# A decode layer's last weight matrix in five transfers instead of nine, and four more of its tiles in the last tile's banks

## The chip, the cores and the metric

One core of a Trainium2 chip runs the whole kernel. The metric is device time in microseconds for one execution, as the median of several. "us" is microseconds throughout.

## The reference

One token of a transformer layer with attention and a gated feed-forward part side by side, all in fp32:

```python
xn = layernorm(x)                                  # x: 1 x 1 x 1024
# A: sliding-window attention over a cache
q = (xn @ wq)                                      # 32 heads of 128
k, v = last 4096 rows of k_cache, v_cache          # 4 kv heads, each for 8 query heads
o = softmax(q k^T * 128 ** -0.5) v
a = o.reshape(1, 1, 4096) @ wo                     # 4096 x 1024
# B: gated feed-forward
h = gelu(xn @ w_gate) * (xn @ w_up)                # 3584 hidden values
b = h @ w_down                                     # 3584 x 1024
return x + a + b
```

There is one row of activations, so every weight is read once and used for one vector: 94.38 MB of weights and cache come in from memory for an output of 1024 numbers.

## The kernel before

All weights and the cache pass through one SBUF buffer, `ring`, of 176 KB in each of the 128 partitions. `pieces` (line 234) lists the transfers in order: kind, which part, the place in the ring in KB, and the size in KB. `pump` (271) issues the next piece on SyncE's queue as soon as no piece that is still in use (`live`) covers its place; `done` frees a place and pumps again. All transfers of weights therefore stand in one queue, in the order of the list. `Program` (36) records every operation with what it reads and writes, and derives the semaphore waits from the overlap of these ranges; a transfer into a place waits for the last readers of exactly that range.

The kinds are q, k, v, g, u, o and d, for wq, the key cache, the value cache, w_gate, w_up, wo and w_down. The change concerns d. w_down's 3584 rows are laid out so that partition p holds rows 28 p to 28 p + 27; tile t is the t-th of these in every partition, a 128 x 1024 block of 4 KB a partition. There are 28 tiles, 0 to 27. Tile t has to be multiplied by column t of the hidden vector and summed over the partitions. There are four ways to take a tile in:

- `tile_on_dve` (644): VectorE multiplies the tile by the column as a per-partition factor and adds it to `out_part` in SBUF (128 x 1024). The sum over the partitions comes later.
- `tiles_on_rows` (611): TensorE, four tiles side by side in four column groups of 32, into all of `acc`, two PSUM banks of 512 columns.
- `tile_on_pe` (626): TensorE, one tile as four matmuls of 256 columns, one in each column group, into `sums`.
- `half_on_pe` (636): TensorE, half a tile as four matmuls of 128 columns, one in each column group, into the first 128 columns of one of `acc`'s banks; half 0 goes to bank 0 and half 1 to bank 1.

`contract` (648) takes one piece: the tiles that are not in `dve_tiles` go to TensorE, those in it to VectorE, and at the end `done` frees the place. `HID_A` to `HID_D` (30 to 33) are the tiles within a piece that VectorE takes. A matmul is recorded as two MATMUL and two LDWEIGHTS records in the trace, so a tile in `sums` is eight records and a half tile is eight as well.

Each engine works through its own instructions in the order in which they are written. The end of the kernel, in that order: both halves of wo and tiles 0 to 11 of w_down by `tiles_on_rows` and VectorE; the sum of `acc` into `out_part`; tiles 12 to 23 by `tile_on_pe` and VectorE; tile 24; `out_part` itself, summed over the partitions by the matrix `unit` in the same way; tile 25, which closes `sums`; VectorE's add of `sums` to x in `x_out`; tile 26 in halves; and then tile 27, whose two halves are transferred separately. After each half of 27 VectorE adds `acc`'s bank to `x_out` and two small transfers store that half of the output.

Of the kernel before, what the change touches and what calls it, by code (L numbers as in the profile page):

```python
# [11 lines left out]
D = 1024  # L12
# [15 lines left out]
HEADS_A = [0, 2, 4, 6, 8, 10, 12, 14]  # L28
HEADS_B = [0, 2, 4, 6, 8, 10, 12, 14]
HID_A = [0, 2, 4, 6, 8]  # L30
HID_B = [1, 3, 5, 7]
HID_C = []
HID_D = [1]


class Program:
# [110 lines left out]
def decode_layer(nc, x, k_cache, v_cache, wq, wo, w_gate, w_up, w_down, out):  # L147
    prog = Program(nc)

    def sbuf(name, *shape):  # L150
        return nc.alloc_sbuf_tensor(name, list(shape), F32)
# [4 lines left out]
    def mm(o, lhsT, rhs, start, stop, parts=None):  # L156
        prog.add(
            "pe", lambda e: e.matmul(o, lhsT, rhs, start=start, stop=stop),  # L158
            [lhsT] + (parts or [rhs]), [o],
        )  # L160
# [16 lines left out]
    def dve(call, reads, writes, engine="dve"):  # L177
        prog.add(engine, call, reads, writes)
# [9 lines left out]
    def add(o, a, b):  # L188
        dve(lambda e: e.tensor_add(o, a, b), [a, b], [o])  # L189
# [38 lines left out]
    def heads_of(a):  # L228
# [12 lines left out]
    ]  # L241
    held = {}

# [35 lines left out]
    def done(*key):  # L279
        del live[key]  # L280
        pump()
# [32 lines left out]
    unit = sbuf("unit", P, 64)  # L314
# [133 lines left out]
    p = rows_sb[:, 0, :]  # L448
# [152 lines left out]
    out_part = part[:, :D]  # L601
# [3 lines left out]
    def column(t):  # L605
        return hz[:, 32 * t:32 * t + 64]
# [4 lines left out]
    def tiles_on_rows(pairs):  # L611

        for at in range(0, len(pairs), 4):
            group = pairs[at:at + 4]
            for f in range(2):
                for k, (z, w) in enumerate(group):
                    c = (state["turn"] + k) % 4
                    first = (c, f) not in state["rows"]
                    state["rows"].add((c, f))
                    mm(  # L620
                        acc[32 * c:32 * c + 32, f, :], z[:, 31:63], w[:, f * NQ:(f + 1) * NQ],
                        first, state["turn"] + k >= state["total"] - 4,
                    )
            state["turn"] += len(group)

    def tile_on_pe(wide, w, stop=False):
        blocks = w.rearrange("p (f c n) -> p c f n", f=2, c=4)
        for c in range(4):
            at = 31 * (c % 2)
            mm(  # L630
                sums[32 * c:32 * c + 32, :].rearrange("p (f n) -> p f n", f=2),
                wide[:, at:at + 32], blocks[:, c], state["fresh"], stop,
            )
        state["fresh"] = False

    def half_on_pe(wide, w, half, first, last):
        for c in range(4):
            at = 31 * (c % 2)
            mm(
                acc[32 * c:32 * c + 32, half, :P],  # L640
                wide[:, at:at + 32], w[:, half * NQ + c * P:half * NQ + (c + 1) * P], first, last,
            )

    def tile_on_dve(z, w):
        add_scaled(out_part, w, z[:, 31:32], state["part"])
        state["part"] = False

    def contract(kind, i, z, dve_tiles, rows):
        w = held[kind, i].rearrange("p (t n) -> p t n", n=D)
        count = w.shape[1]  # L650
        rest = [(z(t), w[:, t, :]) for t in range(count) if t not in dve_tiles]
        if rows:
            tiles_on_rows(rest)
        else:
            for pair in rest:
                tile_on_pe(*pair)
        for t in dve_tiles:
            tile_on_dve(z(t), w[:, t, :])
        done(kind, i)
# [41 lines left out]
    contract("o", 1, lambda t: head(TO + t), HEADS_B, True)  # L701
    contract("d", (0, 12), column, HID_A, True)
    add(out_part, acc[:].rearrange("p a n -> p (a n)"), out_part)
    contract("d", (12, 20), lambda t: column(12 + t), HID_B, False)
    contract("d", (20, 22), lambda t: column(20 + t), HID_C, False)
    contract("d", (22, 24), lambda t: column(22 + t), HID_D, False)
    tile_on_pe(column(24), held["d", (24, 25)])
    tile_on_pe(unit[:], out_part)
    tile_on_pe(column(25), held["d", (25, 26)], True)
    add(x_out[:].rearrange("p f n -> p (f n)"), sums[:], x_out[:].rearrange("p f n -> p (f n)"))  # L710
    for half in range(2):
        half_on_pe(column(26), held["d", (26, 27)], half, True, False)
    stores = out.rearrange("a b (f c n) -> (a b) f c n", f=2, c=4)
    for half in range(2):
        half_on_pe(column(27), held["d", (27, 28)], half, False, True)
# [32 lines left out]
```

## Time and profile before

| | us |
|---|---|
| median of 3 runs | 226.8 |
| lowest and highest | 226.49, 226.84 |
| the profiled execution, in all | 226.83 |
| its span | 225.5 |
| TensorE busy | 87.5 |
| VectorE busy | 143.2 |
| ScalarE busy | 26.3 |

The span reaches from the first to the last instruction of the program; the rest of the time lies around it. PE stands for TensorE's matmuls and PEld for its weight loads, DVE for VectorE, ACT for ScalarE, SP for SyncE, which issues the transfers; SPq is the issuing itself. Times in the profile are counted from the start of the span. In a row of the timeline stand the start, the duration, the engine, the line, the operation, what it writes and reads, its shape, and how often it comes; in brackets stands the idle time of the engine before it and what ended it. Rows of matmuls overlap, so the duration of a row is that of the group. In a row of the windows stand the stretch, its length, the busy time of each engine with its number of instructions (PE, PEld, DVE, ACT, POOL), the clock that was granted to TensorE as a share of the full one, the busy share of the DMA engines, and GB/s.

### The profile page before, as it was taken

What the parts mean: (1) busy time and instruction counts of PE and PEld (TensorE: products, weight loads), DVE (VectorE), ACT (ScalarE), POOL (GpSimd) and SP (SyncE); (2) the same over time, 40 slices, a digit from 0 to 9 for tenths busy, and PEclk for the clock granted to TensorE, in tenths of its full rate; (3) what the DMA queues carried; (4) which work ended last, traced back from release to release, by engine and by line L of the source; (5) the groups of instructions that cost most, each with busy time, mean ns of one, the idle gap of its engine ahead of it and who ended that gap; (6) DMA issues with size and microseconds to landing.
All of it is one profiled execution on the core that took longest, in us unless ns stands there. A gap on an engine that the chain in (4) does not pass through costs nothing.

```text
span 225.5 us, 1396 instructions
## 1 busy us (share of the span) xinstructions
PE 87.5 (39%) x574; PEld 34.8 (15%) x574; DVE 143.2 (64%) x127; ACT 26.3 (12%) x45; POOL 0.7 (0%) x6
## 2 busy tenths in 40 slices
PE   1200000007699007989002537137339204408475
PEld 0100000006263002462000111011002001002131
DVE  7500998499727990000998699869538804938691
ACT  2000000004555001482000300200000000000000
POOL 1000000000000000000000000000000000000000
PEclk9999999999999755999755667857855855965889
DMA  9899899899989999999999998999999999999992
GB/s 373 372 395 535 372 395 535 349 405 478 468 349 426 465 401 503 427 397 471 427 397 392 433 509 387 478 391 491 419 395 488 419 395 413 427 439 442 382 405 111
DMA packets 3317, 94.46 MB, mean 419 GB/s; under 512 B 350, under 2 KB 366, under 8 KB 1008
## 3 DMA queue, kind: packets, MB, share of 16 engines
q1 hardware_dynamic: 3288, 94.38, 97.5%
q8 instruction: 4, 0.07, 0.1%
q10 hardware_dynamic: 24, 0.01, 0.0%
q14 instruction: 1, 0.01, 0.0%
HBM read 94.38 MB, written 0.00 MB: 419 GB/s over the span
## 4 chain that ended last, share of the span: by engine, by line
DMA 65%; DVE 26%; PE 7%; issue 1%; SPq 1%; DVEq 0%
DVE part L213 24%; DMA ring<-in_B_w_down 19%; DMA ring<-in_A_wq 18%; DMA ring<-in_B_w_gate 15%; DMA ring<-in_A_wo 13%; PE acc L158 3%; PE tp L163 2%; PE s_p L158 2%; DVE part L209 1%; SPq L219 1%; DVE rows_sb L186 0%; DVE part L189 0%; DVEq L118 0%; SPq L118 0%
## 5 line engine op out<-in xcount | busy, mean ns | idle before, releaser
L213 DVE SCALAR_TENSOR_TENSOR part<-ring,xz,part 128x3584 f32<-128x3584 f32 (+1 forms) x19 | 78.8, 4148 | 26.6 <-DMA ring<-in_B_w_gate 22.6
L163 PE MATMUL tp<-ident,ring 128*128 128x128 f32 x128 | 20.3, 303 | 44.4 <-DMA ring<-in_A_k_cache 42.8
L213 DVE SCALAR_TENSOR_TENSOR part<-ring,oz,part 128x1024 f32<-128x1024 f32 x15 | 19.3, 1285 | 9.9 <-DMA ring<-in_A_wo 9.4
L172 ACT ACTIVATE ring<-tp 128x512 f32<-128x512 f32 x32 | 18.1, 596 | 58.4 <-PE tp L163 58.0
L163 PEld LDWEIGHTS tp<-ident,ring 128*128 128x128 f32 x128 | 15.0, 152 | 51.2 <-DMA ring<-in_A_k_cache 42.9
L209 DVE TENSOR_SCALAR part<-ring,xz 128x3584 f32<-128x3584 f32 (+1 forms) x3 | 6.5, 2176 | 19.7 <-DMA ring<-in_A_wq 12.1
L158 PE MATMUL acc<-ring,oz 128*32 128x512 f32 x64 | 11.7, 899 | 16.8 <-DMA ring<-in_A_wo 16.8
L213 DVE SCALAR_TENSOR_TENSOR part<-ring,hz,part 128x1024 f32<-128x1024 f32 x10 | 12.8, 1285 | 6.1 <-DMA ring<-in_B_w_down 5.8
L158 PE MATMUL acc<-part,unit 128*32 128x448 f32 (+1 forms) x48 | 7.3, 742 | 22.3 <-DVE part L213 22.3
L158 PE MATMUL o_p<-ring,pT 128*32 128x512 f32 x64 | 11.0, 847 | 7.1 <-DMA ring<-in_A_v_cache 6.5
L158 PE MATMUL acc<-ring,hz 128*32 128x128 f32 (+1 forms) x60 | 8.0, 616 | 10.1 <-DMA ring<-in_B_w_down 10.1
L158 PE MATMUL s_p<-ring,qz 128*32 128x512 f32 x64 | 9.3, 598 | 0.0
L163 PE MATMUL tp<-ident,rows_sb 128*128 128x128 f32 x16 | 3.5, 361 | 12.0 <-ACT rows_sb L172 11.8
L158 PE MATMUL sums<-ring,hz 128*32 128x256 f32 x72 | 6.2, 482 | 4.7 <-DMA ring<-in_B_w_down 4.7
L158 PEld LDWEIGHTS acc<-ring,oz 128*32 128x32 f32 x64 | 2.5, 155 | 26.6 <-DMA ring<-in_A_wo 19.4
L158 PEld LDWEIGHTS acc<-part,unit 128*32 128x32 f32 x48 | 1.4, 126 | 26.4 <-DVE part L213 24.2
L172 ACT ACTIVATE rows_sb<-s_p,negm 128x512 f32<-128x512 f32 x2 | 1.4, 687 | 30.4 <-DVE negm L209 30.4
L158 PEld LDWEIGHTS o_p<-ring,pT 128*32 128x32 f32 x64 | 2.6, 149 | 14.5 <-issue 13.4
L158 PE MATMUL acc<-ring,xz 128*32 128x448 f32 x32 | 4.8, 767 | 0.0
L158 PEld LDWEIGHTS acc<-ring,hz 128*32 128x32 f32 x60 | 2.2, 135 | 15.8 <-issue 14.0
L163 PEld LDWEIGHTS tp<-ident,rows_sb 128*128 128x128 f32 x16 | 2.3, 179 | 15.5 <-ACT rows_sb L172 13.6
L158 PEld LDWEIGHTS sums<-ring,hz 128*32 128x32 f32 x72 | 2.4, 136 | 9.2 <-DMA ring<-in_B_w_down 7.3
(85 smaller groups left out, 47.8 us busy)
## 6 DMA issues: line engine op xcount, KB each, us to landing
ring<-in_B_w_gate SPq DMA_DIRECT2D x2, 7168.0 KB, 31.9
ring<-in_B_w_up SPq DMA_DIRECT2D x2, 7168.0 KB, 33.9
ring<-in_A_k_cache SPq DMA_DIRECT2D x2, 4096.0 KB, 39.7
ring<-in_A_v_cache SPq DMA_DIRECT2D x2, 4096.0 KB, 34.8
ring<-in_B_w_down SPq DMA_DIRECT2D x1, 6144.0 KB, 42.9
ring<-in_B_w_down SPq DMA_DIRECT2D x1, 4096.0 KB, 38.8
ring<-in_B_w_down SPq DMA_DIRECT2D x2, 1024.0 KB, 40.4
ring<-in_B_w_down SPq DMA_DIRECT2D x3, 512.0 KB, 42.0
```

What stands on the lines that cost most here:

```text
L158: "pe", lambda e: e.matmul(o, lhsT, rhs, start=start, stop=stop),
L163: prog.add("pe", lambda e: e.transpose(o, i, eye), [i, eye], [o])
L172: "act", lambda e: e.activation(o, i, func, scale=scale, **kw),
L209: dve(lambda e: e.tensor_scalar(o, i, s1, s2, op0=op0, **kw), reads, [o])
L213: lambda e: e.scalar_tensor_tensor(o, i, factor, other, op0=ALU.mult, op1=ALU.add),
L219: engine, lambda e: e.dma_start(o, i), list(reads), list(writes), dma=True, tag=tag
```

## The change

w_down's pieces are cut anew. Before, they are of 48, 32, 8, 8, 4, 4, 4 and 4 KB a partition, the last in two halves: nine transfers. After, they are of 48, 44, 16 and 4 KB, the last in two halves: five. They cover the same places in the ring. The piece of 44 KB holds tiles 12 to 22, of which VectorE takes two (12 and 14) and TensorE nine, in `sums`; before, VectorE took five of tiles 12 to 23. `out_part` then closes `sums`. Tiles 23 to 26 come as one piece, and go in halves into `acc`'s banks, all four into half 0 and then all four into half 1, ahead of tile 27. Tiles 24 and 25 went into `sums` before, 23 to VectorE, and 26 into `acc`'s banks already.

```diff
-HID_B = [1, 3, 5, 7]
-HID_C = []
-HID_D = [1]
+HID_B = [0, 2]
...
-        ("d", (0, 12), 128, 48), ("d", (12, 20), 0, 32), ("d", (20, 22), 32, 8),
-        ("d", (22, 24), 40, 8), ("d", (24, 25), 48, 4), ("d", (25, 26), 52, 4),
-        ("d", (26, 27), 56, 4), ("d", (27, 28), 60, 4),
+        ("d", (0, 12), 128, 48), ("d", (12, 23), 0, 44), ("d", (23, 27), 44, 16),
+        ("d", (27, 28), 60, 4),
...
-    contract("d", (12, 20), lambda t: column(12 + t), HID_B, False)
-    contract("d", (20, 22), lambda t: column(20 + t), HID_C, False)
-    contract("d", (22, 24), lambda t: column(22 + t), HID_D, False)
-    tile_on_pe(column(24), held["d", (24, 25)])
-    tile_on_pe(unit[:], out_part)
-    tile_on_pe(column(25), held["d", (25, 26)], True)
+    contract("d", (12, 23), lambda t: column(12 + t), HID_B, False)
+    tile_on_pe(unit[:], out_part, True)
     add(x_out[:].rearrange("p f n -> p (f n)"), sums[:], x_out[:].rearrange("p f n -> p (f n)"))
+    wide = held["d", (23, 27)].rearrange("p (t n) -> p t n", n=D)
     for half in range(2):
-        half_on_pe(column(26), held["d", (26, 27)], half, True, False)
+        for t in range(23, 27):
+            half_on_pe(column(t), wide[:, t - 23, :], half, t == 23, False)
```

## The prediction

> **What bounds the kernel now.** I read the page first: its head, the busy shares, the transfer queues and the shares of the chain that ended last.
>
> ```profile
> span 225.5 us, 1396 instructions
> PE 87.5 (39%) x574; PEld 34.8 (15%) x574; DVE 143.2 (64%) x127; ACT 26.3 (12%) x45; POOL 0.7 (0%) x6
> q1 hardware_dynamic: 3288, 94.38, 97.5%
> DMA 65%; DVE 26%; PE 7%; issue 1%; SPq 1%; DVEq 0%
> ```
>
> One queue of transfers keeps the 16 DMA engines 97.5% busy over the whole span. No compute engine is near that; TensorE works for 39% of the time. So the time is the stream of 94.38 MB, plus what still has to be done after its last byte. The chain of waits in order of time shows how short that remainder is:
>
> ```profile
> 180.50 42.73 DMA ring<-in_B_w_down
> 223.23 0.04 issue
> 223.28 0.47 PE acc L158 x8
> 223.75 0.02 issue
> 223.77 0.29 DVE part L189
> ```
>
> The last piece of w_down lands at 223.23. Half a tile on TensorE follows, then one add of 0.29 that ends at 224.06, and 1.4 us later the span ends. The change rewrites just this tail, so I took the timeline of the last 40 us, TensorE's rows first, then VectorE's and the weight loads whose spacing gives TensorE's pace:
>
> ```profile
> 203.63 6.50 PE L158 MATMUL acc<-ring,hz 128*32 128x512 f32 x28 [9.33 <-DMA ring<-in_B_w_down]
> 213.25 4.26 PE L158 MATMUL sums<-ring,hz 128*32 128x256 f32 x48 [3.12 <-DMA ring<-in_B_w_down]
> 218.22 0.64 PE L158 MATMUL sums<-ring,hz 128*32 128x256 f32 x8 [0.71 <-DMA ring<-in_B_w_down]
> 219.49 0.64 PE L158 MATMUL sums<-ring,hz 128*32 128x256 f32 x8 [0.62 <-DMA ring<-in_B_w_down]
> 219.94 0.62 PE L158 MATMUL sums<-part,unit 128*32 128x256 f32 x8
> 220.78 0.64 PE L158 MATMUL sums<-ring,hz 128*32 128x256 f32 x8 [0.21 <-DMA ring<-in_B_w_down]
> 222.03 1.04 PE L158 MATMUL acc<-ring,hz 128*32 128x128 f32 x24 [0.61 <-DMA ring<-in_B_w_down]
> 223.28 0.43 PE L158 MATMUL acc<-ring,hz 128*32 128x128 f32 x8 [0.21 <-DMA ring<-in_B_w_down]
> 203.59 6.57 DVE L213 SCALAR_TENSOR_TENSOR part<-ring,hz,part 128x1024 f32<-128x1024 f32 x5 [4.00 <-DMA ring<-in_B_w_down]
> 213.30 6.57 DVE L213 SCALAR_TENSOR_TENSOR part<-ring,hz,part 128x1024 f32<-128x1024 f32 x5 [1.82 <-DMA ring<-in_B_w_down]
> 213.68 0.20 PEld L158 LDWEIGHTS sums<-ring,hz 128*32 128x32 f32 x4 [0.23 <-issue]
> ...
> 216.24 0.80 PEld L158 LDWEIGHTS sums<-ring,hz 128*32 128x32 f32 x16 [0.23 <-issue]
> ```
>
> Three things are in these rows. First, landings: a wait on w_down ends at 203.6 (tiles 0 to 11), 213.25 (12 to 19), 218.22 (22, 23), 219.49 (24), 220.78 (25), 222.03 (26) and 223.28 (second half of 27). Second, TensorE idles before each and keeps up. Third, it has two paces. A tile in "sums" is eight records, two passes of four that run side by side in the four column groups. From 213.25 to 216.24 a pass takes 2.99 / 7 = 0.427; 24 records then remain of the 48 that end at 217.51, less than 1.3 us for five passes. The windows row by row show why:
>
> ```profile
> 188.98:192.39 3.41, 3.39 (x16) 0.79 (x20) 3.27 (x3) 0.00 (x0) 0.00 (x0) 0.50 1.03 447
> 192.39:195.80 3.41, 1.91 (x20) 0.36 (x12) 3.30 (x4) 0.00 (x0) 0.00 (x0) 1.00 1.00 432
> ...
> 202.62:206.04 3.42, 2.41 (x12) 0.68 (x16) 2.42 (x2) 0.00 (x0) 0.00 (x0) 0.50 0.98 422
> 206.04:209.45 3.41, 3.41 (x17) 0.87 (x12) 3.30 (x4) 0.00 (x0) 0.00 (x0) 0.50 0.98 423
> 209.45:212.86 3.41, 0.68 (x6) 0.00 (x0) 1.93 (x2) 0.00 (x0) 0.00 (x0) 1.00 0.89 377
> 212.86:216.28 3.42, 3.03 (x32) 1.42 (x36) 2.90 (x3) 0.00 (x0) 0.00 (x0) 0.50 1.00 413
> 216.28:219.69 3.41, 2.08 (x36) 0.78 (x32) 3.34 (x3) 0.00 (x0) 0.00 (x0) 1.00 1.02 405
> 219.69:223.10 3.41, 2.55 (x48) 0.85 (x40) 0.60 (x2) 0.00 (x0) 0.00 (x0) 1.00 0.53 202
> ```
>
> The columns that matter are the first, PE busy, and the granted clock (0.50 or 1.00). The clock steps at 192.39, 209.45, 212.86 and 216.28, all on one grid of 3.41 us. A stretch with TensorE busy for 3.03 of 3.42 (89%) is followed by full clock, one with 2.41 (71%) is not; a stretch with 0.68 (20%) is followed by half clock. So every burst after a long wait begins at half clock: the full clock came 3.03 us after the start in the burst of 213.25 (at 216.28), and 5.82 after it in that of 203.63 (at 209.45). In the kernel before, the slow stretch is over well ahead of the last landing.
>
> **The change part by part.**
>
> Transfers. Nine become five. Eight tiles in one transfer land 213.25 - 203.6 = 9.65 after the one before, 1.21 a tile; tiles sent alone land 1.27, 1.29 and 1.25 apart (218.22, 219.49, 220.78, 222.03). The second transfer, now 11 tiles, is therefore whole at 203.6 + 11 x 1.21 = 216.9; taking the pace of the pieces, (218.22 - 213.25) / 4 = 1.24 a tile, 217.25. I take 216.9, since this too is one large transfer. Tiles 23 to 26 land at 216.9 + 4.85 = 221.75, and the last half about 1.25 later, at 223.0: 0.2 earlier than now. That is all that fewer transfers can give, 4 x 0.06. A rule in the Trainium skill, "DMA: Bandwidth & Descriptors", section "Anatomy of one DMA", puts about 2.0 us of fixed cost on each transfer (measured there on GpSimd's path). By it, as an estimate, four fewer would be worth 8 us were they serial; the spacing of 1.25 to 1.29 for 512 KB says that here it runs beside the data of the next.
>
> Issue. SyncE now waits for the reader of tile 10 of the first half of wo before the second transfer, not of tile 6, two VectorE steps of 1.3 later. What is queued behind it:
>
> ```profile
> 170.42 9.21 DVE L213 SCALAR_TENSOR_TENSOR part<-ring,oz,part 128x1024 f32<-128x1024 f32 x7
> 174.37 17.02 SPq L219 DMA_DIRECT2D ring<-in_B_w_down  x8
> ring<-in_B_w_down SPq DMA_DIRECT2D x1, 4096.0 KB, 38.8
> ```
>
> Issue near 177 instead of 174.4 against bytes that cannot flow before 203.6: nothing, with 26 us of cover. Four issues fewer on SyncE: nothing, as none was late.
>
> VectorE. It has two of tiles 12 to 22 instead of five of 12 to 23: 2 x 1.3 = 2.6 from 216.9, done at 219.5. The "unit" matmuls that fold its sum in stand behind nine tiles on TensorE, later than that at any clock below. No cost; but the work it loses goes to TensorE.
>
> TensorE. After the landing at 216.9 it gets nine tiles and the unit tile in "sums" (ten of 256 columns), then eight half tiles for 23 to 26 and two for 27, all of 128 columns. Before, it had only tile 26 and 27 in halves and idle gaps of 0.2 to 0.7 between tiles. At full clock a tile of eight records takes 0.64 alone and a half 0.43 alone; the difference, 0.21, is one half's streaming, so a tile streams 0.43 and a half 0.21 to 0.22, with 0.21 of latency once. (The tile at 219.49 and the unit at 219.94 are 0.45 apart.) All of it at full clock: 10 x 0.43 + 10 x 0.22 = 6.5 us. From 216.9 that ends at 223.4. The stream for 27's second half now ends at 223.28 + 0.22 = 223.5. So even at full clock the new order is only level with the old one: the 0.2 from the transfers is used up.
>
> The clock. TensorE stops near 210.1 (203.63 + 6.50) and waits until 216.9, 6.8 us, which holds at least one whole stretch of 3.41 with no work. The one after 209.45, with 20%, was enough for half clock, so the burst starts at half clock. Each microsecond there does 0.215 / 0.427 of its full-clock work, so it costs 0.495. How long does it last? The traced bounds are 3.03 and 5.82 us. If the grid lay as it does here, the stretch 216.28 to 219.69 would be busy for 82%, between the 71% that failed and the 89% that passed: 2.8 us or 6.2. Nothing in one trace fixes the grid against the landing in another execution, so I take the middle of the two bursts, 4.4 us, and 2.8 and 6.2 as ends. Cost 4.4 x 0.495 = 2.2, ends 1.4 and 3.1. The Trainium skill, "TensorE: Matmul & The Clock Gate", "The HAM clock gate", agrees on the step and its 3413 ns, calls the window free-running (no single trace can show that), and wants at least one busy window. Read as a wholly busy window, an average start would wait 5.1 us, an estimate of 2.5 and a time of 229.3; the 89% stretch that was followed by full clock says that less is enough.
>
> No wait for data is left in it. Tiles 23 to 26 land at 221.75 and are wanted when the ten tiles of "sums" are through, at the earliest 216.9 + 4.3 + 1.4 = 222.6. The halves of 27 land at 222.4 and 223.0 and are wanted 8 x 0.22 = 1.8 later than that, at 224.4. VectorE's add of "sums" follows the unit tile and runs beside the halves.
>
> The end. The two final adds were 0.63 apart and now follow halves 0.22 apart; the first takes 0.29, so the second waits 0.07.
>
> Sum against the profiled execution: the last half's stream ends at 216.9 + 6.5 + 2.2 = 225.6 instead of 223.5, plus 0.07: +2.15 us. The profiled execution took 226.83 in all (span 225.5 and 1.33 around it), 0.03 above the median 226.8. So 226.83 + 2.15 = 229.0 us.
>
> **The rivals.**
>
> TensorE at full clock. If the burst ran at 1.00 from the start, the stream ends at 223.4 for 223.5 and the last add waits 0.07: 226.8, no change. For it: the full clock survived 192.39 to 195.80 with 1.91 us of work. Against it: 20% in 209.45 to 212.86 lost the clock at once, and here the wait is 6.8 us.
>
> The stream still decides (the other side). If TensorE finished "sums" and the eight halves before 223.0, the last landing would end the kernel again, 0.24 earlier: 226.83 - 0.24 = 226.6. That needs the landing of 12 to 22 at or before 216.4, or under 6 us of work where 6.5 is counted at full clock; both would have to differ from the rows. The fixed cost that the Trainium skill states above would be this rival with a larger price, 218.8 by its estimate; the spacing of 1.25 leaves that almost no chance.
>
> The clock never rises in the burst. Then 20 passes of 0.427 and 20 of 0.214 take 12.8 us, 6.3 more: 233. For it only the 5.82 us of the burst at 203.63; every burst that filled one whole stretch got its clock.
>
> **How the numbers follow.** Forecast (TensorE ends the kernel after a half-clock start of 2.8 to 6.2 us): 0.90, time 229.0. Full clock: 0.04, 226.8. The stream decides: 0.03, 226.6. Never full: 0.03, 233. What this kernel's timing can tell from no change is about 0.2%, 0.45 us. Faster 0.03, same 0.04, slower 0.93. The forecast's ends are 226.83 - 0.1 + 0.07 + 1.4 = 228.2 and, with 3.1, 229.9. The later landing of 217.25 adds 0.35 at the top. A share just over 71% that passes (2.4 us of half clock, cost 1.2) takes 0.2 off at the bottom, and 0.1 is left for the rounding of the terms. Range 227.9 to 230.2.
>
> **What would show it.** In the profile after: a wait on w_down that ends near 216.9; a TensorE burst from there without a gap over 0.2 to the last add, 8 to 10 us long; granted clock 0.50 in its first 2.8 to 6.2 us; weight loads 0.43 apart there; the last add released by TensorE and not by a landing; TensorE, not the transfers, in the last 7 us of the chain. Wrong would be: idle TensorE ahead of the last half, a burst at 1.00 from the start, or halves that stream in well over 0.22.

## The result, and the profile after

| | before | after |
|---|---|---|
| median of 5 runs, us | 226.8 | 229.34 |
| lowest and highest | 226.46, 226.84 | 228.68, 229.67 |
| the profiled execution, its span | 226.83, 225.5 | 228.68, 227.3 |

The ratio of after to before is 1.0113, with a 95% interval of 1.0092 to 1.0133: slower by 2.5 us. The times of the kernel after are also wider apart, by 1.0 us instead of 0.4. Line numbers after are two lower: L156 is the helper for matmuls, L187 that for adds.

The head of the page, and the part of the chain of waits that belongs to the tail:

```profile
span 227.3 us, 1483 instructions
q1 hardware_dynamic: 2712, 94.37, 96.6%
```

```profile
176.70 39.81 DMA ring<-in_B_w_down
216.51 0.04 issue
216.56 6.50 PE sums L156 x80
223.05 2.02 PE acc L156 x72
225.07 0.02 issue
225.10 0.51 DVE part L187 x2
```

Before, the chain was in a transfer until 223.23. Now it leaves the transfers at 216.51, and TensorE holds it for the last 8.5 us before the two final adds. The timeline shows the burst without a gap, and the weight loads its two paces:

```profile
216.56 6.07 PE L156 MATMUL sums<-ring,hz 128*32 128x256 f32 x72 [7.82 <-DMA ring<-in_B_w_down]
222.45 0.60 PE L156 MATMUL sums<-part,unit 128*32 128x256 f32 x8
222.88 2.36 PE L156 MATMUL acc<-ring,hz 128*32 128x128 f32 x80
...
216.98 0.20 PEld L156 LDWEIGHTS sums<-ring,hz 128*32 128x32 f32 x4 [0.23 <-issue]
...
219.97 0.20 PEld L156 LDWEIGHTS sums<-ring,hz 128*32 128x32 f32 x4 [0.23 <-issue]
220.40 1.74 PEld L156 LDWEIGHTS sums<-ring,hz 128*32 128x32 f32 x32 [0.23 <-issue]
```

Passes come 0.43 apart until 220.40 (seven steps from 216.98 to 219.97); from there four tiles' weight loads (32) take 1.74, 0.22 a pass. In the windows on this execution's grid (behind the length PE's busy time, behind POOL's column the granted clock):

```profile
210.37:213.79 3.42, 0.00 (x0) 0.00 (x0) 0.73 (x1) 0.00 (x0) 0.00 (x0) 1.00 0.98 422
213.79:217.20 3.41, 0.65 (x8) 0.40 (x12) 0.59 (x1) 0.00 (x0) 0.00 (x0) 0.50 0.90 384
217.20:220.61 3.41, 3.41 (x38) 1.58 (x32) 1.97 (x2) 0.00 (x0) 0.00 (x0) 0.50 0.94 386
220.61:224.03 3.42, 3.42 (x90) 2.35 (x84) 0.42 (x1) 0.00 (x0) 0.00 (x0) 1.00 0.16 56
```

The stretch from 210.37 had no work, so the clock is 0.50 from 213.79; the burst starts at 216.56, fills the stretch from 217.20 whole, and has 1.00 from 220.61: 4.05 us at half clock.

### The profile page after: what moved, and what is told of

The parts are those of the page before. It is cut to its first block, busy times and chain, and to the rows that moved or that the text cites. A ratio compares the mean times of both kernels' runs of the same rounds, so it can differ in the third digit from the quotient of the medians.

```text
span 227.3 us, 1483 instructions
## 1 busy us (share of the span) xinstructions
PE 90.5 (40%) x622; PEld 37.5 (17%) x622; DVE 139.2 (61%) x124; ACT 26.2 (12%) x45; POOL 0.7 (0%) x6
## 4 chain that ended last, share of the span: by engine, by line
DMA 72%; DVE 17%; PE 10%; ACT 1%; issue 0%; DVEq 0%
DMA ring<-in_A_v_cache 18%; DMA ring<-in_B_w_down 18%; DVE part L211 14%; DMA ring<-in_B_w_gate 14%; DMA ring<-in_A_wo 13%; DMA ring<-in_A_wq 10%; PE o_p L156 5%; PE sums L156 3%; DVE part L207 2%; PE acc L156 1%; PE tp L161 1%; ACT rows_sb L170 0%; DVE m L199 0%; ACT pT L170 0%; DVE part L187 0%
## 5 line engine op out<-in xcount | busy, mean ns | idle before, releaser
L156 PE MATMUL acc<-ring,oz 128*32 128x512 f32 x64 | 11.2, 868 | 17.2 <-DMA ring<-in_A_wo 17.2
L156 PE MATMUL acc<-part,unit 128*32 128x448 f32 (+1 forms) x48 | 9.8, 967 | 20.3 <-DVE part L211 20.3
L156 PE MATMUL o_p<-ring,pT 128*32 128x512 f32 x64 | 11.8, 907 | 7.9 <-DMA ring<-in_A_v_cache 7.2
L211 DVE SCALAR_TENSOR_TENSOR part<-ring,hz,part 128x1024 f32<-128x1024 f32 x7 | 9.0, 1284 | 9.7 <-DMA ring<-in_B_w_down 9.5
L156 PE MATMUL acc<-ring,hz 128*32 128x128 f32 (+1 forms) x108 | 7.8, 428 | 8.7 <-DMA ring<-in_B_w_down 8.7
L156 PE MATMUL s_p<-ring,qz 128*32 128x512 f32 x64 | 9.3, 598 | 0.0
L156 PE MATMUL sums<-ring,hz 128*32 128x256 f32 x72 | 6.1, 512 | 7.8 <-DMA ring<-in_B_w_down 7.8
L156 PEld LDWEIGHTS acc<-ring,oz 128*32 128x32 f32 x64 | 2.5, 153 | 26.5 <-DMA ring<-in_A_wo 19.5
L156 PEld LDWEIGHTS acc<-part,unit 128*32 128x32 f32 x48 | 1.8, 159 | 25.8 <-DVE part L211 22.3
L156 PEld LDWEIGHTS acc<-ring,hz 128*32 128x32 f32 x108 | 3.6, 121 | 13.0 <-issue 12.8
L156 PE MATMUL acc<-ring,xz 128*32 128x448 f32 x32 | 5.6, 870 | 0.0
L156 PEld LDWEIGHTS o_p<-ring,pT 128*32 128x32 f32 x64 | 2.8, 159 | 15.6 <-issue 14.5
L156 PEld LDWEIGHTS sums<-ring,hz 128*32 128x32 f32 x72 | 2.8, 147 | 11.5 <-DMA ring<-in_B_w_down 8.7
```

Of the source, the lines that this page charges most:

```text
L211: lambda e: e.scalar_tensor_tensor(o, i, factor, other, op0=ALU.mult, op1=ALU.add),
```

## The experiments

The theory: the large landing lets TensorE idle long enough to lose its clock, and then gives it 6.5 us of full-clock work at once, of which the first 2.8 to 6.2 us run at half clock. Rival A: it is the work that was moved to TensorE (fewer tiles on VectorE, more halves), the clock aside. Rival B: TensorE waits for pieces that land too late. Each kernel below was timed against the kernel before on the same chip (226.81 for e1 to e4, 226.69 for e5, e7, e8 and e9, 226.56 in a single run for e10), and each ratio is to that kernel.

**e1: keep TensorE busy ahead of the landing.**

```diff
     add(out_part, acc[:].rearrange("p a n -> p (a n)"), out_part)
+    for _ in range(6):
+        for c in range(4):
+            mm(s_p[32 * c:32 * c + 32, :], unit[:, 31:63], rows_sb[:, 0, :], True, True)
```

> The changed kernel, with six groups of 24 matmuls in all into an unused bank (no data that is in transfer) behind tiles 0 to 11, so that TensorE does not idle ahead of the large landing. Theory (the half-clock start of the long burst is the cost): granted clock 1.00 over the whole burst, the last passes end 6.5 us after the landing, 226.6 to 227.0 us. Rival A (TensorE simply has more work behind a later landing, the clock aside): no gain, 229.3. Rival B (the large pieces land too late, and TensorE waits for them): no gain, 229.3.

227.9 us, ratio 1.0057 (1.0038 to 1.0076), and two clusters: 227.37, 227.40, 227.46 and 228.34, 228.50, 228.70. So 1.4 of the 2.5 us came back at the median and 1.9 in the lower cluster, where the theory had all of it. The profiled execution (227.46) is of the lower cluster. Its TensorE rows show that the clock was kept, and what was overlooked:

```profile
209.36 5.74 PE L156 MATMUL s_p<-rows_sb,unit 128*32 128x512 f32 x47
216.84 4.09 PE L156 MATMUL sums<-ring,hz 128*32 128x256 f32 x72 [1.74 <-DMA ring<-in_B_w_down]
220.75 0.61 PE L156 MATMUL sums<-part,unit 128*32 128x256 f32 x8
221.73 2.39 PE L156 MATMUL acc<-ring,hz 128*32 128x128 f32 x80 [0.36 <-DMA ring<-in_B_w_down]
```

The nine tiles take 4.09 instead of 6.07, and then TensorE waits for tiles 23 to 26, which land together at 221.7. After that it has ten halves, 2.2 us of streaming, which end at 223.9. In the kernel after, whose burst is slow, this second wait does not show. For the upper cluster the guess was that six groups are too few when the burst of tiles 0 to 11 gets its clock early: they end early, and TensorE idles again. No profile of the upper cluster was taken. e7 tests both.

**e2: the same matmuls, three groups, in the kernel before.**

> The kernel before with three such groups of matmuls behind tiles 0 to 11: what they cost by themselves. Theory: the stream of transfers ends this kernel, TensorE has slack at either clock, 226.8 within 0.3. If the extra matmuls disturb the stream or its landings, slower than 227.1; if the clock held the kernel before back as well, faster than 226.4.

226.8 us, ratio 0.9999 (0.9991 to 1.0008). The three groups cost nothing by themselves. In the profile the clock is at 1.00 from the landing of tiles 12 to 19 (213.24) and back at 0.50 from 219.47 (its rows stand in the last section), and the time is the same: the kernel before has nothing to gain from the clock.

**e3: nine transfers with the new split of work.**

```diff
-        ("d", (0, 12), 128, 48), ("d", (12, 23), 0, 44), ("d", (23, 27), 44, 16),
-        ("d", (27, 28), 60, 4),
+        ... the nine of before ...
+    tiles = [held["d", (22, 24)][:, D:]] + [held["d", (t, t + 1)] for t in range(24, 27)]
+    for t in range(23, 27):
+        for half in range(2):
+            half_on_pe(column(t), tiles[t - 23], half, t == 23, False)
```

> The nine transfers of before with the work split as in the changed kernel (two of tiles 12 to 22 on VectorE, 23 to 26 in halves into acc's banks, tile by tile as they land). Theory: the split alone costs nothing as long as tiles land one by one, since the last landing still ends it, 226.6 to 227.1. Rival A (the split, with five tiles' worth of work moved to TensorE or to halves, is the cost): 228.5 to 229.3.

226.75 us, ratio 1.0 (0.9992 to 1.0009). The split costs nothing by itself: rival A alone falls. Its burst also ran at half clock, from 213.1 to 216.5, but it started 3.6 us earlier (212.98), and the tiles that land one by one leave gaps to catch up in:

```profile
212.98 5.78 PE L156 MATMUL sums<-ring,hz 128*32 128x256 f32 x72 [4.57 <-DMA ring<-in_B_w_down]
...
221.78 1.05 PE L156 MATMUL acc<-ring,hz 128*32 128x128 f32 x24 [0.62 <-DMA ring<-in_B_w_down]
223.05 0.43 PE L156 MATMUL acc<-ring,hz 128*32 128x128 f32 x8 [0.21 <-DMA ring<-in_B_w_down]
```

**e4: five transfers with the old split.**

```diff
-HID_B = [0, 2]
+HID_B = [1, 3, 5, 7]
...
+    tile_on_dve(column(23), wide[:, 0, :])
+    tile_on_pe(column(24), wide[:, 1, :])
+    tile_on_pe(unit[:], out_part)
+    tile_on_pe(column(25), wide[:, 2, :], True)
     for half in range(2):
-        for t in range(23, 27):
-            half_on_pe(column(t), wide[:, t - 23, :], half, t == 23, False)
+        half_on_pe(column(26), wide[:, 3, :], half, True, False)
```

> The five transfers of the change with the work split of before (VectorE takes 13, 15, 17, 19 and 23; 24 and 25 go into sums, 26 in halves). Theory: the burst still starts at half clock at the late landing and VectorE's five tiles end near 223.2, so unit, 25, 26 and 27 follow them: 224.9 for the last stream, 228.3 to 228.8. Rival A (the split is the cost, not the transfers): 226.6 to 227.0.

228.74 us, ratio 1.009 (1.0077 to 1.0103). With the work where it was, the five transfers still cost 1.9 us: here VectorE is the one that starts late, as its timeline and the wait of the unit tile show. TensorE's clock has no part in this loss, for TensorE idles 1.13 us ahead of the unit tile. So what costs is the late landing of many tiles at once, for whichever engine gets them.

```profile
216.72 6.57 DVE L211 SCALAR_TENSOR_TENSOR part<-ring,hz,part 128x1024 f32<-128x1024 f32 x5 [5.46 <-DMA ring<-in_B_w_down]
...
223.34 0.64 PE L156 MATMUL sums<-part,unit 128*32 128x256 f32 x8 [1.13 <-DVE part L211]
```

**e7: as e1, eight groups.**

> The changed kernel with eight groups of extra matmuls behind tiles 0 to 11 instead of six, so that TensorE's idle time ahead of the large landing stays under half a stretch of 3.41 us in every execution. Theory: the two clusters of e1 (227.4 and 228.5) are executions in which the clock was kept and in which it fell again; now it is always kept, 227.3 to 227.6, spread under 0.4. What is left over before (0.6) is TensorE waiting for tiles 23 to 26, which land together at 221.7: ten halves of 0.22 after that. Rival (the upper cluster is something else, for instance the extra matmuls running into the burst): still two clusters, median 227.9 or later.

227.36 us (227.24 to 227.61), ratio 1.0028 (1.0017 to 1.0039). One cluster: the upper one of e1 is gone, and the spread is 0.4 instead of the 1.0 of the kernel after. That e1's upper cluster was the clock is argued from this; no trace shows it. With the clock kept the loss is 0.7 us (against 226.69), so 1.9 of the 2.5 us are back. The windows of the burst, all at 1.00, and TensorE's rows with the wait that is left:

```profile
211.61:215.02 3.41, 3.41 (x40) 1.16 (x35) 0.00 (x0) 0.00 (x0) 0.00 (x0) 1.00 0.80 340
215.02:218.43 3.41, 2.85 (x42) 1.13 (x38) 1.35 (x2) 0.00 (x0) 0.00 (x0) 1.00 0.97 413
218.43:221.85 3.42, 3.09 (x60) 1.58 (x51) 1.49 (x2) 0.00 (x0) 0.00 (x0) 1.00 0.72 283
```

```profile
217.00 4.09 PE L156 MATMUL sums<-ring,hz 128*32 128x256 f32 x72 [0.56 <-DMA ring<-in_B_w_down]
220.91 0.61 PE L156 MATMUL sums<-part,unit 128*32 128x256 f32 x8
221.88 2.39 PE L156 MATMUL acc<-ring,hz 128*32 128x128 f32 x80 [0.36 <-DMA ring<-in_B_w_down]
```

**e8: as e7, with the piece of 23 to 26 cut in two.**

```diff
-("d", (23, 27), 44, 16),
+("d", (23, 25), 44, 8), ("d", (25, 27), 52, 8),
```

Each pair goes into both halves before the next pair.

> As e7, with the piece of tiles 23 to 26 cut into two of 8 KB a partition (six transfers). Theory: tiles 23 and 24 now land 2.4 us earlier and are done before 25 and 26 land, so TensorE ends level with the stream, 226.7 to 227.1, 0.4 to 0.6 less than e7. Rival (the wide piece does not matter, the rest over before is work on TensorE): as e7, 227.4.

226.84 us, ratio 1.0006 (0.9997 to 1.0015), 0.5 less than e7. TensorE no longer waits after the unit tile:

```profile
216.66 4.09 PE L156 MATMUL sums<-ring,hz 128*32 128x256 f32 x72 [1.19 <-DMA ring<-in_B_w_down]
220.57 0.61 PE L156 MATMUL sums<-part,unit 128*32 128x256 f32 x8
221.00 2.37 PE L156 MATMUL acc<-ring,hz 128*32 128x128 f32 x80
```

Rival B is thus a real second part, 0.5 us, which the slow clock covers in the kernel after: there the rows show no wait between the unit tile and the halves. The two pieces without the extra matmuls were not run. The median is level with before, 226.69, so eight groups of extra matmuls do not disturb the transfers either.

**e5: less work in the burst, clock untouched.**

```diff
-HID_B = [0, 2]
+HID_B = [0, 2, 4, 6]
```

> The changed kernel, no extra matmuls, with VectorE taking four of tiles 12 to 22 (12, 14, 16, 18) instead of two. Theory: the burst still starts at half clock for 2.8 to 6.2 us; the two tiles taken away are its last in sums, which mostly run at full clock (0.86), until VectorE's sum at 221.9 becomes the wait: 228.1 to 228.6. Rival (the burst is at half clock throughout, so two tiles are worth 1.7): 227.6. Rival (TensorE's work is not what ends it): 229.3.

228.39 us, ratio 1.007 (1.0056 to 1.0084). That is 0.95 less than the changed kernel, but it is not the price of two tiles on TensorE. In its profile the burst, now shorter, ends in a wait for VectorE's sum of four tiles:

```profile
217.01 4.67 PE L156 MATMUL sums<-ring,hz 128*32 128x256 f32 x56 [6.66 <-DMA ring<-in_B_w_down]
222.36 0.64 PE L156 MATMUL sums<-part,unit 128*32 128x256 f32 x8 [0.68 <-DVE part L211]
217.06 5.25 DVE L211 SCALAR_TENSOR_TENSOR part<-ring,hz,part 128x1024 f32<-128x1024 f32 x4 [5.36 <-DMA ring<-in_B_w_down]
```

VectorE is done at 222.31 (217.06 + 5.25) at any clock, so in this execution fewer tiles on TensorE could not have brought more. The clock was 0.50 for 2.97 us (217.01 to 219.98) and then 1.00, so the rival with half clock throughout falls by the trace. By the line under e10 below, the changed kernel with this landing and this half clock would end TensorE's work at 217.01 + 6.68 + 0.495 x 2.97 = 225.16; here it ends at 225.18 (222.81 + 2.37). The two tiles brought nothing in it, and what a tile in the burst is worth stays open.

**e10: three more profiled executions of the changed kernel.**

> The changed kernel as it is, one profiled execution: when the granted clock rises against the start of the burst. Theory: the grid of 3.41 us is not tied to the kernel, so the half-clock part w of the burst differs from execution to execution between 2.7 and 6.2 us, and the time is 226.7 + 0.495 w (228.7 at the 4.05 us of the first profile). Rival (the spread of the changed kernel's times comes from the transfers): w the same each time, and the landing near 216.5 moves instead.

> The same kernel, a second profiled execution: 226.7 + 0.495 w by the theory, with another w; by the rival the same w and another landing.

> The same kernel, a third profiled execution: 226.7 + 0.495 w by the theory, with another w; by the rival the same w and another landing.

They took 228.04, 229.95 and 229.11. The windows of the first and of the second, around the start of the burst:

```profile
215.96:219.37 3.41, 2.65 (x28) 1.28 (x32) 2.57 (x2) 0.00 (x0) 0.00 (x0) 0.50 0.99 420
219.37:222.78 3.41, 3.41 (x76) 2.10 (x72) 0.18 (x1) 0.00 (x0) 0.00 (x0) 1.00 0.51 190
```

```profile
215.96:219.37 3.41, 2.41 (x24) 1.20 (x28) 2.32 (x2) 0.00 (x0) 0.00 (x0) 0.50 0.95 404
219.37:222.78 3.41, 3.41 (x36) 1.59 (x32) 0.25 (x1) 0.00 (x0) 0.00 (x0) 0.50 0.49 187
222.78:226.20 3.42, 3.42 (x104) 2.77 (x100) 0.42 (x1) 0.00 (x0) 0.00 (x0) 1.00 0.00 0
```

By chance the two lie on the same grid, and they are the sharpest pair of the study. In the first the burst starts at 216.72, fills 78% of the stretch to 219.37 and gets its clock there: 2.65 us at half clock. In the second it starts at 216.96, fills 71%, and gets its clock only at 222.78: 5.82 us. A landing 0.24 later went with an execution 1.9 us longer: 3.17 us more at half clock are worth 1.57, and the landing itself 0.24. In the third the grid lies otherwise, and the half clock lasts 4.6 us:

```profile
216.83 6.33 PE L156 MATMUL sums<-ring,hz 128*32 128x256 f32 x72 [7.55 <-DMA ring<-in_B_w_down]
...
218.00:221.41 3.41, 3.41 (x36) 1.58 (x32) 1.45 (x2) 0.00 (x0) 0.00 (x0) 0.50 0.80 319
221.41:224.82 3.41, 3.41 (x92) 2.48 (x88) 0.42 (x1) 0.00 (x0) 0.00 (x0) 1.00 0.07 22
```

The line 226.7 + 0.495 w gives 228.0, 229.6 and 229.0. The second comes out 0.4 too low, which is about its later landing (216.96 against the 216.56 from which the line was drawn). From the landing to the end of TensorE's last row the four profiled executions take 8.68, 7.99, 9.56 and 8.95 us; that is 6.68 + 0.495 w within 0.01. So the rival's moving landing is there too, at its own price of tenths; the half clock makes the rest of the spread.

**e9: both parts mended.** As e8, with `HID_B = [0, 2, 4]` and the unit tile behind tiles 23 and 24.

> As e8, with VectorE taking three of tiles 12 to 22 and its sum folded in behind tiles 23 and 24. Theory: with the clock kept and no wait for the wide piece the last landing ends the kernel, and that is 0.1 to 0.25 earlier than before for want of three transfers: 226.5 to 226.8. Rival (fewer transfers bring nothing): 226.8; slower than 227.1 if TensorE still ends it.

226.55 us (226.35 to 226.79) against 226.69 of before, ratio 0.9992 (0.9983 to 1.0). That is 0.14 less, about what three transfers fewer are worth by the rows of before (3 x 0.06 = 0.18), but the interval reaches to no change. The profile shows the same size: TensorE's weights for the last half wait for its landing again,

```profile
222.93 0.16 PEld L156 LDWEIGHTS acc<-ring,hz 128*32 128x32 f32 x8 [0.24 <-DMA ring<-in_B_w_down]
```

and from the start of the burst of tiles 0 to 11 (203.44 here, 203.63 before) it is 19.49 us to that, where it was 19.65 before (to 223.28). The chain of waits still runs through TensorE from 216.70 on, so the two end nearly level.

## Why the prediction was right, and where a term was off

The time, 229.34, lies 0.3 above the 229.0 forecast and within the range; the eight executions seen (228.04 to 229.95) fill the range of 227.9 to 230.2 nearly from end to end. Where one execution falls in it depends on the grid of the clock, so that the median of five came within 0.3 of the middle is in part luck.

- The landing: forecast 216.9, 216.56 in the profile after, 216.72 to 216.96 in e10. The step was right: from the start of the burst of tiles 0 to 11 (203.31 after) it is 13.25 us, 11 x 1.20. The whole stream was 0.3 earlier there.
- The burst: forecast at 0.43 a pass at half clock, 0.43 a tile and 0.22 a half at full clock, 6.5 us in all. After has 0.43 a pass; in e7, at full clock, nine tiles and the unit run from 217.00 to 221.5 (4.5 less 0.2 of latency, 10 x 0.43), the ten halves in 2.39 with their latency. One count in the working is wrong and changes nothing: behind 216.24 five passes of four were left, 20 records and not 24.
- Half clock: forecast 4.4 us within 2.8 to 6.2. Measured 4.05, 2.65, 5.82 and 4.6, one of them just under the lower end. That the grid differs between executions is now shown by e10 (steps at 220.61 after, 219.37 and 221.41 in e10). The prediction had it only from the Trainium skill, "TensorE: Matmul & The Clock Gate", "The HAM clock gate", which calls the window free-running. Read as one wholly busy window, that section's rule is stricter than e10's first execution shows, where 78% was enough.
- The other steps: the transfers' gain of 0.24 at most (e9: 0.14), nothing for the issue, VectorE done at 219.2 (216.60 + 2.60, its row in the timeline after), long before the unit tile at 222.45.
- The end: forecast 0.07 for the second add. It is not late, for the two adds take 0.51 together, so they overlap; late are the stores. From the last stream's end (225.0: 222.88 + 2.36 less 0.2 of latency) to the span's end at 227.3 it is about 0.2 us more than before, where it was 2.0 (223.5 to 225.5). The two stores of each queue are now issued one right behind the other, 0.64 for both, where the first was issued well ahead of the second, 0.89 for both:

```profile
225.42 0.64 SPq L217 DMA_DIRECT2D out_y<-part  x2
```

```profile
223.46 0.89 SPq L219 DMA_DIRECT2D out_y<-part  x2
```

  The first row is of after, the second of before. So this term was about 0.2, not 0.07. With it, the landing 0.34 earlier and half clock 0.35 us shorter than forecast (0.17), the sum is 228.6 instead of 229.0, against the profiled 228.68.
- The step that failed is the "full clock" rival's price, 226.8, and with it the sentence that at full clock the new order is level with the old. e7 is that case: 227.36. The working let the 6.5 us run through from 216.9 and checked the landing of 23 to 26 only against the slow burst. At full clock "sums" is done at 221.4, the wide piece lands at 221.7 to 221.9, and ten halves follow it: 0.5, by e8. In e8, where that wait is gone and the clock is kept, the time is the rival's 226.8. The forecast was not touched by it, since there "sums" ends after the landing.
- The rival "the stream still decides" needed other work and another order, as e9 has. The rival "never full" did not occur.

## What to carry to other kernels

When transfers bound a kernel, the size of its last pieces is set by how much work each landing releases: cut them so that what is left to do after each one fits into the time to the next. Cutting w_down into five transfers instead of nine could save 0.1 to 0.25 us of stream and cost 2.5 us of tail, because the engine idled, lost its clock, and then got all its work at once. Price the start of such a burst at half clock, and check each later landing against the fast case as well as the slow one.

## What the runs showed of the hardware

The granted clock stepped only on a grid of 3.41 us whose place differed between executions. A stretch that was busy for 78% (2.65 of 3.41, e10's first execution) raised it, and one of 75% did not (2.55 of 3.42, e5), nor did one of 79% at another place (2.69 of 3.41, e1); one busy for 38% (after) and one for 40% (e2) lost it:

```profile
202.91:206.33 3.42, 2.55 (x13) 0.70 (x17) 2.56 (x2) 0.00 (x0) 0.00 (x0) 0.50 1.04 448
206.33:209.74 3.41, 3.41 (x18) 0.85 (x12) 3.30 (x4) 0.00 (x0) 0.00 (x0) 0.50 1.10 476
```

```profile
193.31:196.72 3.41, 1.29 (x12) 0.12 (x4) 3.30 (x4) 0.00 (x0) 0.00 (x0) 1.00 1.07 461
196.72:200.13 3.41, 0.00 (x0) 0.00 (x0) 2.52 (x2) 0.00 (x0) 0.00 (x0) 0.50 1.07 461
```

```profile
216.06:219.47 3.41, 1.37 (x24) 0.32 (x16) 3.34 (x3) 0.00 (x0) 0.00 (x0) 1.00 1.01 404
219.47:222.89 3.42, 3.40 (x40) 1.76 (x44) 0.81 (x2) 0.00 (x0) 0.00 (x0) 0.50 0.59 226
```

```profile
124.00:127.41 3.41, 2.69 (x16) 0.84 (x8) 1.70 (x1) 1.51 (x2) 0.00 (x0) 0.50 1.00 428
127.41:130.83 3.42, 0.00 (x0) 0.00 (x0) 3.38 (x2) 0.00 (x0) 0.00 (x0) 0.50 1.04 443
```

The first pair is of e5, the second of the kernel after, the third of e2, the fourth of e1. In the thirteen profiles of this case every half-clock stretch that was busy for 80% or more was followed by full clock and none under 76% was; between the two both occur. What decides there is not shown, and the ends of matmuls are modelled in these rows. That the border is narrow enough for 0.24 us of landing to go with 1.9 us of time had not been expected.
